# Attention and two feed-forward layers on one core: the 192-query softmax scaling moved from GpSimd to ScalarE and VectorE, its PSUM copies free to run on either, and every order computed anew

## The chip, the core and the metric

The kernel runs on one core of one Trainium2 chip. A core has a matrix engine (TensorE, PE in the profile), three elementwise engines (VectorE = DVE, ScalarE = ACT, GpSimd = POOL) and a queue, SyncE = SP, that starts DMA transfers. Each engine works through its own instructions strictly in order. The metric is the device time of one execution in microseconds (us); shorter is better.

## The reference

```python
def reference(q, k, v, moe_w_in, moe_w_out, moe2_w_in, moe2_w_out):   # q, k, v: (4, 8, 576, 64)
    scores = q @ k^T / sqrt(64), masked where query block i < key block j (blocks of 64)
    attn = softmax(scores) @ v
    x = attn, heads side by side            # (2304, 512)
    h = x @ w_in                            # 512 -> 2048
    x = (h * tanh(softplus(h))) @ w_out     # 2048 -> 512, "mish"
    h = max(x @ w2_in, 0)
    return (h * h) @ w2_out
```

All of it is float32, and the result is float32.

## The kernel before

**Tiling.** The 2304 tokens are cut into six chunks of 384. Chunks 0 and 1 are the first 192 queries of the four batches (two batches each); chunks 2 to 5 are the other 384 queries of one batch each. A chunk's attention has to be done before the chunk can go through layer one, and that before layer two. This makes 12 passes (a layer and a chunk each) in a fixed sequence. Within a pass the 2048 hidden columns are walked in 16 steps of 128: matrix products into `hp` (line 1063), the activation into `h` by ScalarE (line 1069, with 1088 in the first pass), the split of `h` into two float16 parts `g` (the high one by ScalarE, line 909, or GpSimd, line 910; the low one by VectorE, line 620), then products into four accumulators `acc` (line 1129). The products of the first pass read float32 directly (lines 1083 and 1098).

**Weights.** They arrive as 64-bit words, 1 MB a unit, 32 units (16 for each layer). A unit is decoded by one ScalarE instruction (line 934) and three of VectorE (937, 938, 940), and split into two float16 parts by ScalarE (948 and 909) and VectorE (620). In the first pass, layer one's decode, its split and the attention of chunk 1 run beside the matrix products.

**The 192-query attention** (`attention_lo`, 16 pairs of heads: eight in chunk 0, eight in chunk 1; in the texts a pair is called a head pair). For one of them: TensorE makes the scores (line 842); VectorE masks them and takes the row peaks (846 to 849); ScalarE takes three exponentials with their sums (852); VectorE adds a constant to the sums and takes the reciprocals (855, 857); three instructions of 192, 192 and 64 columns scale the exponentials by these (`scaled`, line 622; line 626 is its GpSimd form); TensorE turns the result round (865 to 868); ScalarE copies it out of PSUM (871); TensorE multiplies by v (880, 881); ScalarE copies that out of PSUM into `xs` (818 in `settle`).

**What sets the order.** While the program is built, a planner (`Sched`) is given every step with a duration in nanoseconds, places them one by one on the engines, and so fixes each engine's list. Some steps may go to one of several engines; the planner takes the one on which it reckons they end first (`choose`, table `ENG`). The instruction lists are then static. Its durations are the numbers in `c_act`, `c_dve`, `c_pool`; `L2_AT`, `S_AT`, `C0_AT`, `A_AT`, `ATT`, `LEAD`, `Sched.URGE`, `Sched.HYST` say from when and in what order of urgency things are wanted.

Of the kernel before, what the change touches and what calls it, by code (L numbers as in the profile page):

```python
# [26 lines left out]
ONE = None  # L27
# [17 lines left out]
LAG = 3  # L45
LOCK = False

# [9 lines left out]
def seg_len(tiles):  # L57
# [8 lines left out]
ENG = {"qkh": A + P, "v": V + P, "va": A, "rebias": A, "wh": A, "xh": A + P, "g1h": A + P, "g2h": A + P, "sq": A + P, "nsq": A,  # L66
       "pn": P, "ph": A, "pl": P + V}
EXTRA, EXTRAP = {"sv": 1, "st": 3}, {}
REBIAS = 2.0 ** -112
KBMAX = 207.4  # L70
DMAR = 290.0

# [4 lines left out]

L2_AT = [85000.0, 5000.0]
LEAD = [117000.0, 49680.0]
C0_AT, C1_AT, A_AT = 40000.0, 85000.0, [[0.0, 20000.0], [70000.0, 90000.0], [95000.0, 150000.0]]  # L80

# [29 lines left out]
class Sched:  # L111
# [15 lines left out]
    SHY = {}  # L127
    CONTEND = 0.5, 100.0, 0.3
    AHEAD = 1500.0
# [47 lines left out]
    def clock(self, t, start):  # L177

        left, now = t.dur, start
        while left > 0:  # L180
            k = int((now + self.PHASE) / self.TICK)
            rate = 1.0 if self.busy.get(k - 1, 0.0) >= self.DUTY * self.TICK else 2.0
            step = min(left * rate, (k + 1) * self.TICK - self.PHASE - now + 1e-3)
            self.busy[k] = self.busy.get(k, 0.0) + step / rate * t.rows
            left -= step / rate
            now += step
        t.dur = now - start
# [250 lines left out]
def c_f32(n):  # L438
    return 2 * max(107.0, 2.5 + n / 1.2)
# [7 lines left out]
def tile_attention_moe(ctx, tc, qk, qp, va, vd, w1, w2, out):  # L447
# [364 lines left out]
    def settle(src, av, n, xs, k, xo, sv):  # L812
# [4 lines left out]
        j = k if n > 192 else 2 * k + (xo > 0)  # L817
        sch.add("ACT", c_act(n, True, 0 if sv is ONE else 1), lambda: nc.scalar.activation(dst(), src(), AF.Copy, scale=scale()),
                r=r, w=[av, (xs, (k, xo))])
        if not whole:  # L820
# [3 lines left out]
    def attention_lo(b, h, x, xo, s_bank, av_bank):  # L824
# [45 lines left out]
        steps.append(sch.add("PE", 4 * 110.0, turn, r=[pf], w=[pp]))  # L870
        sch.add("ACT", c_act(448, True), lambda: nc.scalar.activation(pt.t, pp.t[:, 64:512], AF.Copy), w=[pp, pt])

        def second():
# [8 lines left out]

            step = sch.add("PE", 2 * c_f32(192) + c_f32(64) + 100, mm_av, r=[pt, vs], w=[av])
            step.rows = 0.8
# [38 lines left out]
    def decode(l, k, j):  # L923
# [9 lines left out]
        choose(ENG["rebias"], {  # L933
            "ACT": ("ACT", c_act(n), lambda: nc.scalar.activation(wf.t, high(), AF.Copy, scale=REBIAS), False),
            "POOL": ("POOL", c_pool(n, False), lambda: nc.gpsimd.tensor_scalar(wf.t, high(), REBIAS, 1.0, ALU.mult, ALU.mult), False),
# [500 lines left out]
```

## Time and profile before

| | |
|---|---|
| device time, median of 3 runs | 972.25 us (971.27 to 973.7) |
| the profiled execution: its device time | 972.16 us |
| its span, first to last instruction | 970.1 us |
| mean granted TensorE clock in it | 0.975 of full speed |
| busy: PE, DVE, ACT, POOL | 921.4, 598.0, 630.4, 131.6 us |

The span is 2.06 us shorter than the execution's own device time; that part lies around the instructions. A line "L626" is line 626 of the kernel. Busy time of PE is modelled from records of pipelined products, so a busy PE need not be a PE at full speed; the granted clock tells how fast it was allowed to run (1.00 is 2.4 GHz, 0.50 is 1.2 GHz).

### The profile page before, as it was taken

To read this page: it belongs to the slowest core of one execution; us is meant where nothing else is said; L and a number is where in the kernel's file an instruction comes from. 1 tells how busy PE (TensorE), PEld (TensorE's weight loads), DVE (VectorE), ACT (ScalarE), POOL (GpSimd) and SP (SyncE) were. 2 spreads that over 40 slices of the span, in tenths; PEclk is the share of its full clock that TensorE was granted. 3 is DMA by queue.
4 is the path that set the end of the run, shared out by engine and by line. 5 is a ranking of instruction groups with operands and counts; after the bars stand their busy time and mean duration, and the time that the engine had idled before them with its cause. 6 is when DMAs were issued, how large, how long until landed. Compare 5 with 4: busy or idle time off the path is not lost. (4 is left out here: it accounts for less than half of the span.)

```text
span 970.1 us, 15652 instructions
## 1 busy us (share of the span) xinstructions
PE 921.4 (95%) x5732; PEld 543.0 (56%) x5732; DVE 598.0 (62%) x1405; ACT 630.4 (65%) x1152; POOL 131.6 (14%) x192
## 2 busy tenths in 40 slices
PE   8688899899899999999999999999999999999997
PEld 7445465465455565555655655655556666666664
DVE  3767679999986757866685386677762341231211
ACT  5567898777776757798688677576784343353442
POOL 3212001123220111201221011011300100000000
PEclk9689989899999999999999999999999999999999
DMA  8467664685586655857444535676553221223222
GB/s 313 162 224 255 238 227 165 220 297 190 169 165 163 174 148 133 189 150 162 127 104 122 115 116 143 161 176 151 148 129 95 66 87 44 71 70 122 98 66 98
DMA packets 135725, 146.78 MB, mean 151 GB/s; under 512 B 105184, under 2 KB 110304, under 8 KB 131552
## 3 DMA queue, kind: packets, MB, share of 16 engines
q1 hardware_dynamic: 135648, 145.78, 52.1%
q8 instruction: 45, 0.74, 0.3%
q14 instruction: 32, 0.26, 0.1%
HBM read 106.43 MB, written 14.16 MB: 124 GB/s over the span
## 5 line engine op out<-in xcount | busy, mean ns | idle before, releaser
L1129 PE MATMUL acc<-g,ws 128*128 128x384 f16 x2112 | 431.6, 327 | 6.0 <-DVE g L620 3.9
L1129 PEld LDWEIGHTS <-ws 128*128 128x128 f16 x2112 | 204.6, 98 | 145.0 <-issue 9.1
L620 DVE SCALAR_TENSOR_TENSOR g<-h,cst,g 128x384 f16<-128x384 f32 x176 | 108.9, 621 | 208.1 <-ACT g L909 173.0
L1069 ACT ACTIVATE h<-hp,cst 128x384 f32<-128x384 f32 x176 | 101.1, 578 | 169.0 <-PE hp L1063 166.0
L1063 PE MATMUL hp<-x,first 128*128 128x384 f16 x960 | 201.2, 327 | 2.4 <-ACT h L1069 2.3
L1063 PE MATMUL hp<-x,late 128*128 128x384 f16 x864 | 180.8, 328 | 0.0
L1063 PEld LDWEIGHTS <-first 128*128 128x128 f16 x960 | 91.7, 98 | 66.4 <-issue 8.1
L1063 PEld LDWEIGHTS <-late 128*128 128x128 f16 x864 | 81.7, 98 | 58.1 <-issue 6.8
L910 POOL TENSOR_SCALAR g<-h,cst 128x384 f16<-128x384 f32 x77 | 60.7, 788 | 347.1 <-PE acc L1129 128.7
L726 ACT ACTIVATE pad<-pab,st,sq 128x320 f32<-128x320 f32 (+2 forms) x96 | 67.3, 703 | 30.0 <-DVE st L721 29.3
L620 DVE SCALAR_TENSOR_TENSOR pb<-pad,st,pb 128x384 f16<-128x384 f32 (+2 forms) x96 | 70.8, 749 | 17.8 <-ACT pb L744 16.4
L744 ACT ACTIVATE pb<-pad,st 128x384 f16<-128x384 f32 (+2 forms) x96 | 64.7, 713 | 15.4 <-ACT pad L726 4.9
L909 ACT ACTIVATE g<-h,cst 128x384 f16<-128x384 f32 x99 | 60.7, 613 | 19.5 <-PE acc L1129 17.7
L1083 PE MATMUL hp<-xs,first 128*128 128x384 f32 x128 | 56.1, 533 | 2.4 <-ACT h L1088 2.4
L1063 PE MATMUL hp<-x,ws 128*128 128x384 f16 x288 | 57.4, 326 | 0.0
L718 DVE TENSOR_REDUCE st<-pab 128x2 f32<-128x640 f32 (+2 forms) x48 | 49.9, 1040 | 3.9 <-PE pab L710 3.0
L1074 ACT ACTIVATE h<-h 128x384 f32<-128x384 f32 x86 | 44.0, 517 | 1.4
L1016 POOL TENSOR_SCALAR x<-xs,cst 128x384 f16<-128x384 f32 x30 | 23.3, 790 | 155.3 <-DVE cst L904 144.1
L626 POOL TENSOR_SCALAR pt<-pt,st 128x192 f32<-128x192 f32 (+1 forms) x48 | 26.6, 572 | 126.4 <-DVE st L857 72.0
L710 PE MATMUL pab<-q 64*128 64x320 f16 (+3 forms) x384 | 39.7, 308 | 2.2 <-DVE q L620 1.0
L1098 PE MATMUL acc<-h,late 128*128 128x384 f32 x96 | 39.3, 507 | 0.0
L1063 PEld LDWEIGHTS <-ws 128*128 128x128 f16 x288 | 27.0, 98 | 20.1 <-issue 2.9
(206 smaller groups left out, 1071.8 us busy)
## 6 DMA issues: line engine op xcount, KB each, us to landing
ws<-wspill SPq DMA_DIRECT2D x100, 512.0 KB, 3.7
raw<-in_w_dram SPq DMA_DIRECT2D x22, 1024.0 KB, 5.1
pad<-in_w_dram SPq DMA_DIRECT2D x10, 1024.0 KB, 4.9
wspill<-wn SPq DMA_DIRECT2D x18, 512.0 KB, 3.1
qk<-in_qp_dram SPq DMA_DIRECT2D x16, 480.0 KB, 4.1
vs<-in_va_dram SPq DMA_DIRECT2D x16, 320.0 KB, 4.2
out_dram<-ev SPq DMA_DIRECT2D x24, 192.0 KB, 2.0
vs<-in_qk_dram SPq DMA_DIRECT2D x10, 320.0 KB, 5.4
```

What stands on the lines that cost most here:

```text
L620: return sch.add("DVE", c_dve(n) + 62 * ap, lambda: nc.vector.scalar_tensor_tensor(dst(), a(), s() if ap else s, c(), op0, op1), r=r, w=w, ...
L710: nc.tensor.matmul(out=pp.t[:, hd, o:o + k1 - k0], lhsT=qh.t[rows, u, a:a + 128], rhs=qh.t[rows, w, nq + k0:nq + k1], start=p == 0, stop=p ...
L718: sch.add("DVE", c_dve(2 * (o1 - o0)), lambda: nc.vector.reduce_max(both(st, j, r0), pp.t[r0:, :, o0:o1], axis=AX.X), w=[(pp, 0), (st, j)])
L726: sch.add("ACT", c_act(o1 - o0, True, 3), lambda hd=hd: nc.scalar.activation(pf[hd].t[r0:, k0:k0 + o1 - o0], pp.t[r0:, hd, o0:o1], AF.Exp, ...
L744: sch.add("ACT", c_act(n, False, 1), lambda pb=pb, pv=pv, s=s: nc.scalar.activation(pb.t[:, 0:i + 1, 0, :], pv(), AF.Copy, scale=s()), r=[ ...
L909: "ACT": ("ACT", c_act(n, False, 1), lambda: nc.scalar.activation(dst(0), src(), AF.Copy, scale=s()), False),
L910: "POOL": ("POOL", c_pool(n, False), lambda: nc.gpsimd.tensor_scalar(dst(0), src(), s(), 1.0, ALU.mult, ALU.mult), False),
L1063: nc.tensor.matmul(out=hp.t[:, 0:n], lhsT=w.t[:, f % 2, a, 128 * k:128 * k + 128], rhs=x.t[:, c, k, 0:n], start=k == 0 and i == 0, stop=k ...
L1069: sch.add("ACT", c_act(n, True, 1), lambda: nc.scalar.activation(h.t[:, 0:n], hp.t[:, 0:n], (AF.Mish, AF.Relu)[l], scale=hs()), r=[(cst, ( ...
L1074: "ACT": ("ACT", c_act(n), lambda: nc.scalar.activation(hv(), hv(), AF.Square), False),
L1083: nc.tensor.matmul(out=hp.t[:, 0:n], lhsT=wf.t[:, 512 * (f % 2) + 128 * k:512 * (f % 2) + 128 * k + 128], rhs=xs.t[:, k, 0:n], start=k == ...
L1129: nc.tensor.matmul(out=acc.t[:, 0:n], lhsT=wo.t[:, f % 2, a, 128 * m:128 * m + 128], rhs=g.t[:, c, 0:n], start=f == 0 and i == 0, stop=f = ...
```

## The change

Three kinds of edit. First, `scaled` may no longer use GpSimd: table entry `pn` goes from GpSimd to ScalarE or VectorE. The two PSUM copies of the 192-query attention (`ptc`: the turned probabilities, 448 columns; `set`: the result, 192 columns) were ScalarE's alone and go through `copy`, which may choose VectorE. Second, numbers of the planner's model change: how VectorE and GpSimd hinder each other (`LOCK`, `CONTEND`), the DMA rate it reckons with, and a few durations. Third, the numbers that say when things are wanted were replaced, so that every engine's list is another.

```diff
-LOCK = False
+LOCK = True
...
-       "pn": P, "ph": A, "pl": P + V}
+       "pn": A + V, "set": A + V, "ptc": A + V, "ph": A, "pl": P + V}
...
-DMAR = 290.0
+DMAR = 360.0
...
-LEAD = [117000.0, 49680.0]
+LEAD = [111400.0, 111770.0]
...
-    CONTEND = 0.5, 100.0, 0.3
+    CONTEND = None
...
-        sch.add("ACT", c_act(n, True, 0 if sv is ONE else 1), lambda: nc.scalar.activation(dst(), src(), AF.Copy, scale=scale()),
-                r=r, w=[av, (xs, (k, xo))])
+        if sv is ONE:
+            copy(ENG["set"], n, dst, src, [], [av, (xs, (k, xo))], True)
+        else:
+            sch.add("ACT", c_act(n, True, 1), lambda: nc.scalar.activation(dst(), src(), AF.Copy, scale=scale()), r=r, w=[av, (xs, (k, xo))])
...
-        sch.add("ACT", c_act(448, True), lambda: nc.scalar.activation(pt.t, pp.t[:, 64:512], AF.Copy), w=[pp, pt])
+        copy(ENG["ptc"], 448, lambda: pt.t, lambda: pp.t[:, 64:512], [], [pp, pt], True)
...
-Sched.SHY={'DVE':1.5}
+Sched.SHY={}
...
-C0_AT = 27210.0
-A_AT = [[0.019, 18240.0], [55700.0, 114970.0]]
+C0_AT = 15160.0
+A_AT = [[0.013, 6840.0], [14100.0, 93900.0]]
...
-S_AT = [[38920.0, 4110.0], [19910.0, 4050.0]]
-Sched.URGE = 77120.0
+S_AT = [[39730.0, 3690.0], [23550.0, 3520.0]]
+Sched.URGE = 83480.0
```

Counted over the whole program, the 48 scaling instructions become 30 of VectorE (22 of 192 columns, 8 of 64) and 18 of ScalarE (10 and 8). Of the 16 copies of 448 columns VectorE gets 7, of the 16 of 192 columns 5. ScalarE's table loads go from 60 to 68. GpSimd's other work, all of which stands behind the scalings in its list, goes from 134 instructions to 115. No product of TensorE is added or taken away but two of the 13 that only fill its start.

The lists are another from the start, and three places matter. Lines after 820 stand two higher in the changed kernel. The first place is VectorE while the last head pairs of chunk 0 go through (`st` holds a head pair's sums and reciprocals, `pt` its probabilities, `first`, `late`, `raw` belong to weights that are decoded). Before:

```order
L940 SCALAR_TENSOR_TENSOR first_71<-raw0_67,first_71 128x1024
L847 TENSOR_REDUCE st_8_388<-spare_133 128x2
L848 TENSOR_REDUCE st_8_388<-spare_133 128x1
L849 TENSOR_SCALAR st_8_388<-st_8_388 128x3
L937 TENSOR_SCALAR late_70<-late_70 128x1024
L855 TENSOR_SCALAR st_7_368<-st_7_368 128x3
L938 SCALAR_TENSOR_TENSOR late_70<-raw1_68,late_70 128x1024
L857 RECIPROCAL st_7_368<-st_7_368 128x3
```

and in the changed kernel:

```order
L942 SCALAR_TENSOR_TENSOR first_71<-raw0_67,first_71 128x1024
L857 TENSOR_SCALAR st_6_305<-st_6_305 128x3
L598 COPY xs_0_260<-acc3_2_351 128x192
L859 RECIPROCAL st_6_305<-st_6_305 128x3
L939 TENSOR_SCALAR late_70<-late_70 128x1024
L627 TENSOR_SCALAR pt_128<-pt_128,st_6_305 128x192
L627 TENSOR_SCALAR pt_128<-pt_128,st_6_305 128x64
L857 TENSOR_SCALAR st_7_320<-st_7_320 128x3
L848 MEMSET spare_133 64x128
L859 RECIPROCAL st_7_320<-st_7_320 128x3
L940 SCALAR_TENSOR_TENSOR late_70<-raw1_68,late_70 128x1024
```

The scalings (L627) and copies (L598) now stand in VectorE's list between the weights' decode, and a wide decode row no longer stands between the sums and the reciprocal of the last head pair of chunk 0 (`st_7`).

The second place is TensorE at the start of the first pass (`spare` is a PSUM buffer of the attention, `xs_0` is chunk 0 as the first pass reads it). Before, up to the first product of the pass:

```order
L880 MATMUL spare_133<-pt_128,pb_127 64x192 x2
L881 MATMUL spare_133<-pt_128,pb_127 128x64
L842 MATMUL spare_133<-vs_129 128x192 x2
L842 MATMUL spare_133<-vs_129 128x64
L880 MATMUL spare_133<-pt_128,pb_127 64x192 x2
L881 MATMUL spare_133<-pt_128,pb_127 128x64
L1083 MATMUL hp0_131<-xs_0_281,first_71 128x384
```

and in the changed kernel:

```order
L867 MATMUL acc2_1_290<-ident_136,pt_128 128x128
L868 MATMUL acc2_1_290<-ident_136,pt_128 128x128
L869 MATMUL acc2_1_290<-ident_136,pt_128 128x2x64
L870 MATMUL acc2_1_290<-ident_136,pt_128 128x128
L882 MATMUL acc3_3_403<-pt_128,pb_127 64x192 x2
L883 MATMUL acc3_3_403<-pt_128,pb_127 128x64
L882 MATMUL spare_133<-pt_128,pb_127 64x192 x2
L883 MATMUL spare_133<-pt_128,pb_127 128x64
L1085 MATMUL hp0_131<-xs_0_260,first_71 128x384
```

Ten head pairs have their scores and nine are finished ahead of the first product of the pass before the change; with it nine have their scores and eight are finished. One pair of chunk 1 moves behind that product.

The third place is VectorE at the first `g` of the second pass (`wf`, `wn`, `late` are layer two's weights). Before:

```order
L955 TENSOR_SCALAR wst_895<-spare 128x2
L940 SCALAR_TENSOR_TENSOR wf<-raw_68,wf 128x1024
L956 TENSOR_SCALAR wst_895<-wst_895 128x2
L620 SCALAR_TENSOR_TENSOR g_1222<-h_1161,cst_1065,g_1222 128x384
L620 SCALAR_TENSOR_TENSOR late<-wf,us_1186,late 128x1024
L904 TENSOR_SCALAR us_1216<-wst_895 128x1
```

and in the changed kernel:

```order
L957 TENSOR_SCALAR wst_890<-spare 128x2
L942 SCALAR_TENSOR_TENSOR wf<-raw_68,wf 128x1024
L620 SCALAR_TENSOR_TENSOR g_1259<-h_1177,cst_1112,g_1259 128x384
L620 SCALAR_TENSOR_TENSOR g_1261<-h_1208,cst_1112,g_1261 128x384
L620 SCALAR_TENSOR_TENSOR g_1263<-h_1216,cst_1112,g_1263 128x384
L620 SCALAR_TENSOR_TENSOR wn_66<-wf,us_1164,wn_66 128x1024
```

Counted from the start of the list, 23 units of weights are decoded and 20 split ahead of this `g` before, 26 and 23 with the change; four reductions of 384 columns (L1108) and four others that stood ahead of it stand behind it.

## Rows read from the trace of the kernel before

**Rows 1.** Busy time of each engine in five stretches; columns as the first line says.

```profile
...
core 0: us, PE busy (x) PEld busy (x) DVE busy (x) ACT busy (x) POOL busy (x), PEclk, DMA share, GB/s
0.00:44.20 44.20, 31.79 (x164) 24.70 (x165) 22.28 (x70) 24.64 (x79) 13.33 (x37) 0.81 0.71 251
44.20:174.80 130.60, 116.57 (x412) 67.82 (x412) 100.47 (x208) 102.65 (x168) 17.02 (x23) 0.92 0.61 217
174.80:280.20 105.40, 96.72 (x592) 54.76 (x592) 101.29 (x215) 79.46 (x128) 26.59 (x26) 0.95 0.68 217
280.20:403.60 123.40, 117.92 (x850) 67.62 (x847) 88.52 (x219) 82.90 (x174) 19.42 (x26) 1.00 0.64 158
403.60:970.00 566.40, 558.42 (x3726) 328.08 (x3720) 285.40 (x696) 340.73 (x606) 55.29 (x80) 1.00 0.44 115
```

**Rows 2.** Timeline of PE: start us, us, what, and idle time before it with its releaser.

```profile
...
27.71 0.43 PE L881 MATMUL acc<-pt,pb 128*128 128x64 f32 x2
34.14 0.47 PE L865 MATMUL acc<-ident,pt 128*128 128x128 f32 x1 [5.99 <-POOL pt L626]
...
44.23 1.59 PE L1083 MATMUL hp<-xs,first 128*128 128x384 f32 x2
```

**Rows 3.** Timeline of VectorE ahead of that stall.

```profile
...
31.18 0.16 DVE L855 TENSOR_SCALAR st<-st 128x3 f32<-128x3 f32 x1
31.30 1.23 DVE L938 SCALAR_TENSOR_TENSOR late<-raw,late 128x1024 uint32<-128x1024 uint32 x1
32.44 0.17 DVE L857 RECIPROCAL st<-st 128x3 f32<-128x3 f32 x1
```

**Rows 4.** Timeline of GpSimd, its first six scalings and a later six.

```profile
...
11.08 2.35 POOL L626 TENSOR_SCALAR pt<-pt,st 128x192 f32<-128x192 f32 x6 [9.47 <-DVE st L848]
...
32.80 4.47 POOL L626 TENSOR_SCALAR pt<-pt,st 128x192 f32<-128x192 f32 x6 [7.03 <-DVE st L855]
```

**Rows 5.** Busy time in windows of 10 us.

```profile
...
20.00:30.00 10.00, 7.90 (x56) 5.33 (x54) 5.64 (x15) 6.92 (x21) 1.43 (x5) 0.98 0.35 132
30.00:40.00 10.00, 4.26 (x15) 2.31 (x15) 7.47 (x15) 5.75 (x15) 4.47 (x6) 0.53 0.70 243
40.00:50.00 10.00, 9.06 (x26) 5.80 (x27) 5.74 (x12) 5.27 (x11) 0.00 (x0) 0.62 0.58 208
50.00:60.00 10.00, 6.39 (x17) 3.42 (x16) 7.56 (x11) 6.23 (x10) 3.84 (x3) 0.72 0.73 256
```

**Rows 6.** Groups of VectorE by form: busy us, mean ns of one, idle before.

```profile
...
L938 DVE SCALAR_TENSOR_TENSOR wf<-raw,wf 128x1024 uint32<-128x1024 uint32 x11 | 14.0, 1268 | 0.0
L940 DVE SCALAR_TENSOR_TENSOR wf<-raw,wf 128x1024 uint32<-128x1024 uint32 x11 | 13.6, 1235 | 0.0
L620 DVE SCALAR_TENSOR_TENSOR wn<-wf,us,wn 128x1024 f16<-128x1024 f32 x10 | 13.1, 1310 | 0.0
...
L937 DVE TENSOR_SCALAR first<-first 128x1024 uint32<-128x1024 uint32 x8 | 5.7, 717 | 2.1 <-ACT first L934 2.1
...
L847 DVE TENSOR_REDUCE st<-spare 128x2 f32<-128x384 f32 x9 | 4.9, 542 | 0.1
...
L1108 DVE TENSOR_REDUCE xm<-xs 128x1 bf16<-128x384 f32 x4 | 2.2, 546 | 0.0
...
L848 DVE TENSOR_REDUCE st<-spare 128x1 f32<-128x64 f32 x9 | 1.9, 212 | 0.3 <-PE spare L881 0.3
```

**Rows 7.** Groups of GpSimd by form.

```profile
...
L626 POOL TENSOR_SCALAR pt<-pt,st 128x192 f32<-128x192 f32 x32 | 18.1, 579 | 126.4 <-DVE st L857 72.0 <-ACT h L1088 20.3 <-DVE wst L956 12.0
```

**Rows 8.** Waits of VectorE in the first pass: us in total, times, longest us.

```profile
...
DVE spare L846 <- PE spare L881: 12.9, 6, 4.7
```

**Rows 9.** Waits of PE in the first pass, same columns.

```profile
...
PE spare L867 <- POOL pt L626: 1.7, 2, 1.3
```

**Rows 10.** Groups of ScalarE by form.

```profile
...
L726 ACT ACT_TABLE_LOAD x22 | 28.2, 1283 | 6.1 <-DVE cst L899 3.5 <-DVE st L721 2.3
...
L818 ACT ACTIVATE xs<-spare 128x192 f32<-128x192 f32 x12 | 3.9, 329 | 12.0 <-PE spare L949 4.7 <-DVE st L847 3.0 <-DVE spare L846 1.9
```

More of the change, by code (lines that the diff above doesn't have):

```diff
@@ L181, in clock @@
             k = int((now + self.PHASE) / self.TICK)
-            rate = 1.0 if self.busy.get(k - 1, 0.0) >= self.DUTY * self.TICK else 2.0
+            rate = 1.0 if k > 2 and self.busy.get(k - 1, 0.0) >= self.DUTY * self.TICK else 2.0
             step = min(left * rate, (k + 1) * self.TICK - self.PHASE - now + 1e-3)
@@ L881, in mm_av @@
                 nc.tensor.matmul(out=av.t[:, 128:192], lhsT=vs.t[:, 128:256], rhs=pt.t[:, 0:64], start=False, stop=True)
-            step = sch.add("PE", 2 * c_f32(192) + c_f32(64) + 100, mm_av, r=[pt, vs], w=[av])
+            step = sch.add("PE", c_f32(192) + c_f32(64) + 200, mm_av, r=[pt, vs], w=[av])
             step.rows = 0.8
@@ L933, in decode @@
         choose(ENG["rebias"], {
-            "ACT": ("ACT", c_act(n), lambda: nc.scalar.activation(wf.t, high(), AF.Copy, scale=REBIAS), False),
+            "ACT": ("ACT", c_act(n) + 90.0, lambda: nc.scalar.activation(wf.t, high(), AF.Copy, scale=REBIAS), False),
             "POOL": ("POOL", c_pool(n, False), lambda: nc.gpsimd.tensor_scalar(wf.t, high(), REBIAS, 1.0, ALU.mult, ALU.mult), False),
@@ L947, in split @@
         sq, us, sc = (R[x].new() for x in ("wsq", "us", "sc"))
-        sch.add("ACT", c_act(n) + 190.0, lambda: nc.scalar.activation(sq.t, wf.t, AF.Square, scale=2.0 ** -13, accum_out=us.t[:, 1:2]), r=[wf], w=[sq, (us, 1)])
+        sch.add("ACT", c_act(n) + 93.0, lambda: nc.scalar.activation(sq.t, wf.t, AF.Square, scale=2.0 ** -13, accum_out=us.t[:, 1:2]), r=[wf], w=[sq, (us, 1)])
         step = sch.add("PE", 110.0, lambda: nc.tensor.matmul(out=sc.t[:, 0:1], lhsT=onesq, rhs=us.t[:, 1:2].bitcast(BF16)[:, 1:2], start=True, stop=True),
@@ L1352 @@
 ATT = [[2, 2, 0, 0.0, 1.2], [3, 2, 1, 1.1, 2.6], [4, 5, 7, 0.5, 2.2], [5, 5, 8, 2.0, 3.6]]
-L2_AT = [89170.0, 2960.0]
+L2_AT = [92220.0, 2850.0]
 W_AT = [[[4300.0, 4600.0], [47800.0, 6800.0]]]
-C0_AT = 27210.0
-A_AT = [[0.019, 18240.0], [55700.0, 114970.0]]
-ATT = [[2, 2, 0, 0.0, 1.309], [3, 2, 1, 0.832, 1.394], [4, 5, 7, 0.015, 2.865], [5, 5, 8, 0.0, 4.407]]
+C0_AT = 15160.0
+A_AT = [[0.013, 6840.0], [14100.0, 93900.0]]
+ATT = [[2, 2, 0, 0.021, 1.144], [3, 2, 1, 0.943, 1.494], [4, 5, 7, 0.0, 4.142], [5, 5, 8, 0.027, 4.334]]
 Sched.SLACK = 0.445
-Sched.HYST = 21950.0
+Sched.HYST = 25790.0
 def setup():
```

## The prediction

> **What bounds the kernel now.** I read the stretches first [rows 1]. They are cut at the first product of the first pass (44.2 us), the first activation of the second pass (174.8), a step in the middle of the third pass (280.2) and the start of the fifth (403.6). In the last stretch TensorE is busy 558.4 of 566.4 us at a granted clock of 1.00: there it alone sets the time, and the change adds no product to it. From 280.2 to 403.6 it is busy 117.9 of 123.4, also at 1.00. So the end of the kernel stands at a nearly fixed distance behind 280.2, and what can be won or lost lies ahead. In the third stretch VectorE is busy 101.3 of 105.4 us, 96%, and TensorE 96.7: VectorE is the limit. In the second nobody is full: VectorE 100.5 and ScalarE 102.7 of 130.6 us, TensorE 116.6 by its records, at 0.92. The first 44.2 us are the emptiest: VectorE 22.3, ScalarE 24.6.
>
> Then I read the timeline where the head is emptiest. TensorE ends a product at 28.14 (27.71 and 0.43) and starts the next at 34.14, after 5.99 us of waiting for a scaling on GpSimd [rows 2]. The reader is to see who was late there: not GpSimd alone. VectorE adds the constant to the sums at 31.18, decodes weights for 1.23 us, and only then takes the reciprocal, at 32.44 [rows 3]; GpSimd starts at 32.80. But then six scalings take it 4.47 us, where its first six took 2.35 [rows 4]. The hole has a second price: the granted clock reads 0.98 in the 10 us before it, then 0.53, 0.62 and 0.72 [rows 5], near the lower of the two levels, 1.2 and 2.4 GHz.
>
> **The change part by part.** The sum is made for one point, the one at 280.2 us, where VectorE is the limit: its time is VectorE's work up to there plus VectorE's idle time up to there. Before, work is 22.28 + 100.47 + 101.29 = 224.0 us, so idle time is 56.2: 21.9 in the head, 30.1 in the first pass, 4.1 in the third stretch [rows 1].
>
> *Work added to VectorE.* 30 scalings and 12 copies. A scaling of the very kind (one tensor, one scalar per row, buffer to buffer) stands in the trace with 1024 columns at 0.717 us [rows 6] and with 3 columns at 0.16 [rows 3]; on the line between them 192 columns are 0.26 and 64 are 0.19, so 22 x 0.26 + 8 x 0.19 = 7.2 us. Bounds: 30 x 0.16 = 4.8, and 30 x 0.579, what GpSimd took on the wide ones [rows 7], = 17.4. I take the line, since the engine and kind of operation are the same. For a read of PSUM, 64 columns are 0.212 and 384 are 0.542 [rows 6], so 192 are 0.34, 448 are 0.61, and the copies 5 x 0.34 + 7 x 0.61 = 6.0 us (2.5 if each went at the 64-column row; 7.3 if each at 0.61). The rows overlap: the one that starts at 31.30 and lasts 1.23 ends 0.09 after the next has started [rows 3]; 42 instructions take 42 x 0.09 = 3.8 off. Net 13.2 - 3.8 = 9.4 us.
>
> *Work that is only moved.* Three units of weights (decode 0.717 + 1.268 + 1.235, split 1.310, together 4.5 us each [rows 6]) go from behind the second pass's first g to ahead of it, and eight reductions (four of them 0.546 each) the other way. Both are over by 280.2 in either list. The units' loads and spills, 1.5 MB each, join a stretch whose DMA share is 0.61 [rows 1], so 4.5 MB more over some 130 us, 35 GB/s on 217, has room. By 280.2 the new list also has five more instructions of the next attention done (384 to 640 columns; by the line of the PSUM reads about 3.5 us) and TensorE has 15 more products behind it. The last stretch has 558.42 us for 3726 products [rows 1], 0.15 each, so these are a credit of 2.2 us.
>
> *Idle time taken away.* In the head a scaling now follows its reciprocal on the same engine, or goes to ScalarE: the way through GpSimd is gone, and with it 4.47 us for two head pairs. The last pair of chunk 0 no longer has a decode row between sums and reciprocal. And one head pair less stands ahead of the first pass. VectorE has the copies and scalings to fill its gaps with. I take half of the head's 21.9 us: 11; bounds 6 and 22. In the first pass 12.9 of VectorE's 30.1 idle us are six waits for TensorE to make room for the next scores [rows 8], and TensorE in turn waits for GpSimd's scalings (1.7 us at one line, the longest of several [rows 9]). With the hole gone and the clock up these shrink, and VectorE has more in its list. Bounds: 30, as now, and 10 (the third stretch's 4% of some 130 us is 5; the ends of the pass add to it). The middle is near 21, and I take that. The third stretch keeps 4.
>
> *Waits added.* A scaling on VectorE waits for ScalarE's exponentials through its reciprocal, and behind it stand decode rows, for which the weights' split and the float32 products of the first pass wait. On ScalarE 18 scalings come (0.329 us for a 192-column copy of PSUM [rows 10], so about 6) and 12 copies go (about as much by the same row and the wider ones). Its 8 more table loads, 8 x 1.283 = 10.3 us [rows 10], lie mostly behind 280.2, where it is idle 40.5 of 123.4 and 225.7 of 566.4 us [rows 1]; that idle time hides them. If it did not, they would cost up to 10.3; I charge 1.5. The two filling products that go stand ahead of everything; I cost them at nothing, and at 0.15 us a product they could not be worth more than 0.3.
>
> *Sum.* 224.0 + 9.4 + 3.5 + (11 + 21 + 4) = 272.9 against 280.2 is -7.3; credit -2.2; table loads +1.5: -8.0. The span of 970.1 becomes 962.1, and with the 2.06 around it the execution is **964.2 us**. The profiled execution's 972.16 is the median of the runs (972.25) within 0.1.
>
> *A rule of the skill beside it.* The two groups of six scalings, 2.35 and 4.47 us, differ by what VectorE did meanwhile: in the second it decodes [rows 3, 4]. The Trainium skill (SBUF — State Buffer, section "Who interferes with whom") says that VectorE, in its two-port modes or with two operands from SBUF, and GpSimd exclude each other for a whole instruction. By that rule the trace agrees on GpSimd's side, VectorE would get time back as well (the rival "More" below), and a scaling on VectorE would block GpSimd where that has work at the time; in the new list all its other work stands later.
>
> **The rivals.**
>
> *Slower: VectorE's list becomes the bound of the first pass.* VectorE takes 9.4 us more in order, each scaling stands ahead of decode rows, and a late exponential then holds up decode, split and the products that wait for them. For it: VectorE and ScalarE are both near 78% there already, and list order has cost them the rest. Against: 30.1 us of slack. Each idle us of the first pass is one us of time: 21 gives 964.2, 29 gives 972, and from 32 on it is slower by over 0.3%. With 36, 979 us.
>
> *No change: the way through GpSimd was not the cause.* The hole of 6 us was opened by VectorE's late sums and reciprocal; GpSimd came 0.36 us after it [rows 3]. If the head keeps some 18 of its 21.9 idle us, because the new list also has decode rows between, the time is 964 + 7 = 971.
>
> *More: the head and first pass both close up.* If idle time falls to 8 and 12 us, it is 3 + 9 = 12 us less, 952. For it speaks the lost clock: three windows at 0.53, 0.62 and 0.72 hold 19.7 us of busy TensorE [rows 5], about 7 us of which (4.26 x 0.47 + 9.06 x 0.38 + 6.39 x 0.28) a full clock would have spared. VectorE rows that no longer share their time with GpSimd's would do it too: if VectorE lost as much as GpSimd did, 48 x (0.579 - 2.35/6) = 9 us, 955.
>
> **Chances.** The forecast (958 to 969) 0.48, more 0.16, no change 0.19, slower 0.17. 0.3%, 2.9 us, is about what a measurement of this kernel can tell from no change. Faster by over that: 0.64; within: 0.19; slower: 0.17. The likeliest is 964; the range reaches from 954 to 977.
>
> **What would show it.** Right: no wait of TensorE over 3 us between 20 and 40 us; the first product of the first pass near 36 instead of 44.23 us; a granted clock over 0.8 from 30 to 60; VectorE busy over 80% from there to the second pass, and over 95% up to the point that was at 280.2; a DVE scaling of 192 columns near 0.26 us. Wrong: VectorE idle over 30 us between the first product of the first pass and the second pass, waiting for ScalarE's exponentials or TensorE's scores; a scaling near 0.5 us; or TensorE waits behind 403.6 that were not there, by ScalarE's table loads.

## The result, and the profile after

The changed kernel takes 956.28 us (median of 4 runs, 954.85 to 959.01) against 972.63 for the kernel before on the same chip: a ratio of 0.9836, 95% interval 0.9807 to 0.9865. It is faster by 16 us. The prediction said 964.2, with a range of 954 to 977. The profiled execution took 954.89 us, its span is 953.1 and its mean granted clock 0.991.

The five stretches, cut at the same steps as in [rows 1], as the windows view has them for the changed kernel:

```profile
...
core 0: us, PE busy (x) PEld busy (x) DVE busy (x) ACT busy (x) POOL busy (x), PEclk, DMA share, GB/s
0.00:29.53 29.53, 23.04 (x146) 18.05 (x146) 20.34 (x78) 20.29 (x73) 1.06 (x10) 1.00 0.95 349
29.53:158.20 128.67, 111.62 (x425) 66.82 (x425) 116.29 (x247) 118.86 (x196) 2.11 (x2) 0.95 0.71 257
158.20:262.50 104.30, 99.44 (x627) 56.59 (x627) 95.49 (x229) 78.54 (x135) 18.49 (x20) 0.98 0.63 189
262.50:384.50 122.00, 117.07 (x845) 68.28 (x841) 86.06 (x215) 84.89 (x173) 15.11 (x19) 1.00 0.65 161
384.50:953.10 568.60, 555.25 (x3698) 326.32 (x3696) 277.87 (x681) 347.83 (x612) 49.90 (x74) 1.00 0.42 113
```

The step that stood at 280.2 us is now at 262.5. From there to the end it is 690.6 us, before 970.1 - 280.2 = 689.9. So all of the gain lies ahead of that point (the step is the same activation of the third pass in every kernel). VectorE's work up to it is 20.34 + 116.29 + 95.49 = 232.1 us, before 224.0. Its idle time, span less busy in each of the three stretches, is 9.2 + 12.4 + 8.8 = 30.4, before 21.9 + 30.1 + 4.1 = 56.2.

The timeline of TensorE where [rows 2] showed the hole of 6 us. The longest wait between 20 and 40 us is 0.79; the first product of the first pass starts at 29.53 instead of 44.23:

```profile
...
22.37 0.55 PE L882 MATMUL acc<-pt,pb 128*64 128x192 f32 x4 [0.79 <-DVE pt L598]
...
29.53 0.86 PE L1085 MATMUL hp<-xs,first 128*128 128x384 f32 x2
```

The windows of 10 us that answer to [rows 5]. The clock is 1.00 in all of them, and VectorE is busy 8.86 us at 20 to 30, where it was 5.64. The last but one number is the DMA engines' share:

```profile
...
20.00:30.00 10.00, 7.81 (x52) 5.12 (x51) 8.86 (x26) 8.82 (x30) 0.00 (x0) 1.00 1.04 397
30.00:40.00 10.00, 9.23 (x39) 5.53 (x38) 8.47 (x18) 8.31 (x15) 0.00 (x0) 1.00 0.78 297
40.00:50.00 10.00, 9.49 (x31) 5.49 (x30) 7.79 (x16) 9.42 (x16) 0.00 (x0) 1.00 0.93 326
50.00:60.00 10.00, 10.00 (x43) 6.27 (x42) 9.25 (x16) 9.44 (x16) 0.00 (x0) 1.00 0.86 326
```

The new rows among the groups of VectorE (busy us, mean ns of one), with a decode row for comparison with [rows 6]:

```profile
...
L942 DVE SCALAR_TENSOR_TENSOR wf<-raw,wf 128x1024 uint32<-128x1024 uint32 x11 | 13.7, 1248 | 0.0
...
L627 DVE TENSOR_SCALAR pt<-pt,st 128x192 f32<-128x192 f32 x22 | 6.3, 314 | 0.1
...
L598 DVE COPY pt<-spare 128x448 f32<-128x448 f32 x5 | 3.1, 623 | 0.8 <-PE spare L951 0.8
...
L627 DVE TENSOR_SCALAR pt<-pt,st 128x64 f32<-128x64 f32 x8 | 2.0, 256 | 0.0
...
L598 DVE COPY xs<-spare 128x192 f32<-128x192 f32 x4 | 1.4, 355 | 1.1 <-PE spare L883 0.8 <-PE spare L951 0.3
```

The scalings that went to ScalarE take 461 and 342 ns there.

VectorE's largest wait in the first pass (us, times, longest), which answers to [rows 8]: 5.7 us where there were 12.9.

```profile
...
DVE spare L848 <- PE spare L883: 5.7, 6, 3.2
```

### The profile page after: what moved, and what is told of

It reads as the page before. It is cut to its first block, busy times and chain, and to the rows that moved or that the text cites. A ratio compares the mean times of both kernels' runs of the same rounds, so it can differ in the third digit from the quotient of the medians.

```text
span 953.1 us, 15648 instructions
## 1 busy us (share of the span) xinstructions
PE 906.4 (95%) x5730; PEld 536.1 (56%) x5730; DVE 596.1 (63%) x1447; ACT 650.4 (68%) x1185; POOL 86.7 (9%) x125
## 5 line engine op out<-in xcount | busy, mean ns | idle before, releaser
L1065 PE MATMUL hp<-x,first 128*128 128x384 f16 x960 | 196.8, 326 | 0.6 <-DVE cst L1033 0.3
L912 POOL TENSOR_SCALAR g<-h,cst 128x384 f16<-128x384 f32 x70 | 49.6, 710 | 360.7 <-PE acc L1131 147.8
L911 ACT ACTIVATE g<-h,cst 128x384 f16<-128x384 f32 x106 | 65.0, 615 | 12.7 <-PE acc L1131 11.7
L1085 PE MATMUL hp<-xs,first 128*128 128x384 f32 x128 | 52.8, 504 | 0.0
L1076 ACT ACTIVATE h<-h 128x384 f32<-128x384 f32 x91 | 47.1, 517 | 1.3
L1018 POOL TENSOR_SCALAR x<-xs,cst 128x384 f16<-128x384 f32 x24 | 20.6, 872 | 249.7 <-DVE cst L1054 154.1
L726 ACT ACT_TABLE_LOAD x25 | 32.1, 1283 | 15.7 <-DVE st L721 10.8
```

Of the source, the lines that this page charges most:

```text
L726: sch.add("ACT", c_act(o1 - o0, True, 3), lambda hd=hd: nc.scalar.activation(pf[hd].t[r0:, k0:k0 + o1 - o0], pp.t[r0:, hd, o0:o1], AF.Exp, ...
L911: "ACT": ("ACT", c_act(n, False, 1), lambda: nc.scalar.activation(dst(0), src(), AF.Copy, scale=s()), False),
L1065: nc.tensor.matmul(out=hp.t[:, 0:n], lhsT=w.t[:, f % 2, a, 128 * k:128 * k + 128], rhs=x.t[:, c, k, 0:n], start=k == 0 and i == 0, stop=k ...
L1076: "ACT": ("ACT", c_act(n), lambda: nc.scalar.activation(hv(), hv(), AF.Square), False),
L1085: nc.tensor.matmul(out=hp.t[:, 0:n], lhsT=wf.t[:, 512 * (f % 2) + 128 * k:512 * (f % 2) + 128 * k + 128], rhs=xs.t[:, k, 0:n], start=k == ...
```

## The experiments

Twelve kernels, each timed against the kernel before on its own chip, where that took 971.92 us (e1 to e4), 971.38 (e5 to e8) and 972.97 (e9 to e12). The changed kernel was timed only beside the 972.63 above, so a comparison with it goes across chips. "First product" is the start of the first product of the first pass; the last column is the place of the step that stood at 280.2. These two are from the profiled execution, which need not be the median one.

| kernel | median us | ratio to before, 95% interval | first product | step |
|---|---|---|---|---|
| before | 972.63 | | 44.2 | 280.2 |
| after | 956.28 | 0.9836 (0.9807 to 0.9865) | 29.5 | 262.5 |
| e1: lists of before, scalings on VectorE | 964.08 | 0.9938 (0.9917 to 0.9959) | 43.9 | 271.3 |
| e2: lists of after, scalings on GpSimd | 976.6 | 1.0052 (1.0028 to 1.0076) | 33.7 | 281.9 |
| e3: after, GpSimd busy beside it | 962.14 | 0.9924 (0.9898 to 0.995) | 33.4 | 270.1 |
| e4: before, 60 filling products | 969.62 | 0.9977 (0.9959 to 0.9995) | 42.5 | 279.0 |
| e5: after, copies on ScalarE | 962.81 | 0.9914 (0.9886 to 0.9943) | 33.0 | 266.7 |
| e6: after, the wanted-when numbers of before | 971.42 | 0.9994 (0.9977 to 1.0011) | 31.2 | 276.5 |
| e7: before, the new choice of engines alone | 978.36 | 1.0061 (1.0041 to 1.0081) | 31.8 | 268.6 |
| e8: before, 105 filling products | 972.33 | 0.9999 (0.9983 to 1.0015) | 43.4 | 279.9 |
| e9: before, decode rows behind the chain | 974.95 | 1.0017 (1.0 to 1.0034) | 46.0 | 282.4 |
| e10: e1 and e9 together | 967.11 | 0.9952 (0.993 to 0.9974) | 46.9 | 274.5 |
| e11: before, 185 filling products | 971.9 | 0.9992 (0.9978 to 1.0007) | 43.8 | 280.4 |
| e12: after, the same shift at its second hole | 963.6 | 0.99 (0.987 to 0.9929) | 32.0 | 271.5 |

**e1 and e2: the engine and the lists apart.** Each instruction keeps its place; only the engine that scales is another, in e1 in the lists of before:

```diff
-        choose(ENG["pn"], {
+        t = choose(ENG["pn"], {
...
+        swap.append((t, lambda: nc.vector.tensor_scalar(v(), v(), s(), None, ALU.mult)))
...
     seq = sch.run(order)
+    for t, fn in swap:
+        t.fn = fn
```

e2 does the same with GpSimd's form (`nc.gpsimd.tensor_scalar`) in the lists of after. Expected of e1:

> The lists of before, but the 48 scalings are VectorE's, each at the place in the order at which GpSimd's stood. Theory A (the way through GpSimd is what cost): the 6 us hole of TensorE at 28 us shrinks to 4 or less, the clock falls less, 962 to 968 us. Theory B (the new lists are what gained, the engine is secondary): within 3 us of before, 970 to 975, because VectorE's list still has the decode rows in front; or slower, since VectorE has 8 us more to do in lists that were not planned for it.

Of e2:

> The lists of after, but all 48 scalings are GpSimd's, each at the place in the order at which VectorE's or ScalarE's stood. Theory A: most of the gain is lost, 966 to 973 us, with TensorE waiting for scalings of 0.4 to 0.75 us. Theory B: 955 to 960 us, because the lists keep the decode rows out of the way.

Measured: the engine alone gives 8 us in the old lists (e1). The new lists with the scalings on GpSimd cost 5 (e2; its 12 copies are still VectorE's, so this is not the lists quite alone, and e1 has all 48 scalings on VectorE, where the changed kernel has 18 on ScalarE). Together they give 16: with the new lists the engine is worth 20. TensorE's timeline of e1 shows that the hole stays as long as it was although GpSimd has no scaling left:

```profile
...
34.29 0.44 PE L868 MATMUL acc<-ident,pt 128*128 128x128 f32 x1 [5.89 <-DVE pt L628]
```

VectorE's timeline of e1 shows what took GpSimd's place. The reciprocal is taken at 32.56, as before (32.44), but then a decode row stands in the list, and the scalings start at 33.83, where GpSimd had started at 32.80 [rows 4]:

```profile
...
32.70 1.22 DVE L943 SCALAR_TENSOR_TENSOR late<-raw,late 128x1024 uint32<-128x1024 uint32 x1
33.83 0.70 DVE L628 TENSOR_SCALAR pt<-pt,st 128x192 f32<-128x192 f32 x3
```

The first pass of e1 in the windows view:

```profile
...
43.90:167.60 123.70, 113.78 (x412) 67.07 (x412) 104.28 (x229) 102.84 (x169) 2.60 (x2) 0.93 0.64 230
```

Of the 8.9 us by which e1 is ahead at the step, 6.9 come from the first pass, 123.7 us against 130.6 [rows 1], 1.7 from the third stretch and 0.3 from the head. In e2 the first product comes at 33.7, and from 20 us to there TensorE's longest wait is 1.19 us: in the new lists the hole is closed even with GpSimd. But the first pass takes 144.6:

```profile
...
33.70:178.30 144.60, 120.04 (x424) 69.71 (x425) 114.60 (x230) 117.03 (x190) 23.77 (x26) 0.90 0.63 222
```

and TensorE's waits in it name GpSimd's scalings, 11.5 us in these three lines alone:

```profile
...
PE spare L871 <- POOL pt L628: 4.9, 6, 1.1
PE spare L872 <- POOL pt L628: 4.6, 4, 2.0
...
PE spare L870 <- POOL pt L628: 2.0, 3, 1.1
```

VectorE's idle time in the four kernels, us, worked out as above from windows cut at the same steps:

| | head | first pass | third stretch | its work |
|---|---|---|---|---|
| before | 21.9 | 30.1 | 4.1 | 224.0 |
| e1 | 17.2 | 19.4 | 2.7 | 231.9 |
| e2 | 15.7 | 30.0 | 8.4 | 227.8 |
| after | 9.2 | 12.4 | 8.8 | 232.1 |

The engine takes 10.7 us of VectorE's idle time out of the first pass in the old lists and 17.6 in the new ones, for 7.9 and 4.3 us more work up to the step. The first pass itself gets shorter by 6.9 (130.6 to 123.7) and 15.9 us (144.6 to 128.7).

**e3: what GpSimd's work does to VectorE.** After, with a scaling on GpSimd of a buffer that nobody reads, beside each of the 48:

```diff
+        beside[t] = lambda: nc.gpsimd.tensor_scalar(idle[:, 0:n], idle[:, 0:n], s(), 1.0, ALU.mult, ALU.mult)
...
             t.fn()
+            if t in beside:
+                beside[t]()
```

> After, and beside each scaling GpSimd scales a buffer of its own of the same size that nobody reads (48 rows more for GpSimd, no wait for them). If GpSimd's rows take time from VectorE's: VectorE's decode and scaling rows in the first 160 us get longer, 4 to 9 us in all, and the time rises to 959 to 965. If they do not: 955 to 958, and the decode rows keep their 1.22 us.

Measured: 962.14, some 6 us over after, with no wait that names those rows. The groups of VectorE in e3:

```profile
...
L947 DVE SCALAR_TENSOR_TENSOR first<-raw,first 128x1024 uint32<-128x1024 uint32 x5 | 6.1, 1225 | 0.0
...
L627 DVE TENSOR_SCALAR pt<-pt,st 128x192 f32<-128x192 f32 x22 | 7.3, 359 | 0.1
...
L627 DVE TENSOR_SCALAR pt<-pt,st 128x64 f32<-128x64 f32 x8 | 2.6, 327 | 0.0
```

The decode rows with two inputs keep their duration: 1225 ns in this group, 1217 in the same group of after. Not each of them has a GpSimd row beside it, so I also counted row by row in the trace of e3: the 10 that overlap one of GpSimd's scalings take 1.232 us in the mean, the other 34 take 1.227. GpSimd pays: its scalings of 192 columns take 1.28 us beside a row of VectorE with two inputs of 1024 columns (9 of them), 0.52 otherwise (23). VectorE's scalings grow from 314 to 359 and from 256 to 327 ns, 22 x 0.045 + 8 x 0.071 = 1.6 us. VectorE's work up to the step is 235.1, 3.0 more, its idle time 35.0, 4.6 more. Of that 2.7 are in the head, where the clock fell:

```profile
...
20.00:30.00 10.00, 8.23 (x38) 5.79 (x35) 7.85 (x23) 6.95 (x26) 5.84 (x9) 0.62 1.01 378
30.00:40.00 10.00, 10.00 (x32) 5.43 (x31) 6.73 (x16) 8.04 (x16) 2.71 (x5) 0.69 0.54 182
```

1.6 us of longer scalings are shown. Why the head lost 3.9 us is not: it lost its clock there, and which small delay came first I did not separate. The head of one and the same program moves too: in e12, which is after up to some 100 us, the first product came 2.5 us later than in after.

**e4, e8, e11: the clock behind the hole.** Before, with filling products in front of the turn that TensorE waits for: 60 and 105, then 185 to cover the hole. e8 and e11 write a free bank; in e4 the bank was one that TensorE first had to wait for, 3.8 us.

```diff
+            if t is turns[7]:
+                for _ in range(185):
+                    nc.tensor.matmul(out=hps[1][:, 0:64], lhsT=ones, rhs=ones[:, 0:64], start=True, stop=True)
             t.fn()
```

> Before, with 60 small products that nobody reads put into TensorE's list in front of the turn of the eighth head pair, where it sat idle for 6 us. If the clock that fell there is a large part of the price: granted clock near 1.00 from 30 to 60 us, 3 to 7 us faster than before, 966 to 970. If waits alone set the head: within 2 us of before.

> Before, with 105 small products that nobody reads in front of the turn of the eighth head pair, now into a PSUM bank that is free there, so that they do not wait for anybody (the 60 of the earlier run waited 3.8 us first). If the clock is a large part of the price of the hole: granted clock over 0.9 from 30 to 60 us, the hole as long as before, 965 to 969 us. If the clock costs little there, since the other engines are waited for anyway: 969 to 972.

> Before, with 185 filling products into a free bank in TensorE's hole of 6 us (105 of them had lasted 3.23 us); no list is changed otherwise. If the hole's second price, the clock that falls behind it, is what costs the time: clock over 0.85 from 30 to 50 and 965 to 968. If the clock falls because of the thin work that follows, or costs little: 0.6 to 0.7 there as before and 970 to 973.

Measured: e4 2 us faster, with its clock at 0.67 to 0.68 from 30 to 60, so these 2 us are not the clock's; e8 and e11 no change. In e8 the 105 left 2.92 us of the hole and the clock at 0.62 to 0.70. In e11 the hole is filled, and these are its windows, to be held against [rows 5]:

```profile
...
20.00:30.00 10.00, 9.75 (x141) 7.60 (x138) 5.71 (x16) 7.34 (x22) 1.50 (x5) 1.00 0.36 126
30.00:40.00 10.00, 7.02 (x120) 4.95 (x116) 7.73 (x15) 5.79 (x16) 4.46 (x6) 0.81 0.72 243
40.00:50.00 10.00, 9.52 (x28) 6.13 (x29) 6.13 (x11) 5.58 (x14) 0.00 (x0) 0.68 0.61 218
50.00:60.00 10.00, 6.52 (x16) 3.71 (x15) 6.74 (x11) 5.45 (x8) 3.85 (x3) 0.66 0.65 244
```

The clock is 0.81 instead of 0.53 at 30 to 40, about as before in the 20 us behind, and the first product comes at 43.8 instead of 44.2. So the hole's second price, "about 7 us", was not there to be had by closing the hole: most of it was reckoned for 40 to 60 us, and there the clock stays low with the hole filled. What a full clock from 40 to 60 would give is not shown, since no fill brought it about.

**e9, e10: taking the decode out of the chain.** In before (e9) and in e1 (e10), the wide rows of VectorE and ScalarE between the scores and the turn of that head pair go behind the turn, with what depends on them:

```diff
+    for p in (7,):
+        first, last = turns[p]
+        i, j = seq.index(first), seq.index(last)
+        late, now = [], []
+        for t in seq[i:j + 1]:
+            own = first.idx <= t.idx <= last.idx
+            wide = t.eng in ("DVE", "ACT") and t.dur > 600.0
+            behind = any(d in late for d in t.deps | t.after)
+            (late if not own and (wide or behind) else now).append(t)
+        seq[i:j + 1] = now + late
```

> The lists of before, the scalings on GpSimd as before; only the wide rows (decode, over 0.6 us) that VectorE and ScalarE have between the scores and the turn of the eighth head pair, the one for which TensorE waits 6 us, are put behind that turn, with what depends on them. Theory, the list made the hole: some 4 to 5 us of decode rows lie in that pair's chain, so the hole of 6.0 us falls under 2, the first product of the first pass comes near 40 (43 to 44 before), the granted clock is over 0.8 from 30 to 50, and the time is 965 to 969 against 972. Rival, the way through GpSimd made it: the hole keeps over 4 us and the time 971 to 973.

> The same shift of the decode rows, with the scalings of before's lists emitted on VectorE, which by itself gave 964.1. If closing the hole and taking the scalings off GpSimd are two separate gains: 958 to 961. If they are one and the same, or what the hole gives is lost again in the first pass as with the new lists and GpSimd: 963 to 966.

Measured: e9 is not faster, and neither theory held (974.95; e10, at 967.11, lies 1 us outside both of its ranges). The wait for the scalings falls from 5.99 to 2.16 us, but TensorE then waits 7.36 for a product that the weights' split needs:

```profile
...
29.89 0.47 PE L867 MATMUL acc<-ident,pt 128*128 128x128 f32 x1 [2.16 <-POOL pt L626]
...
38.63 0.16 PE L952 MATMUL spare<-us,onesq 128*128 128x1 bf16 x1 [7.36 <-ACT wsq L951]
38.66 0.45 PE L867 MATMUL spare<-ident,pt 128*128 128x128 f32 x1
...
45.97 0.95 PE L1086 MATMUL hp<-xs,first 128*128 128x384 f32 x1
```

ScalarE's timeline in e9 shows why: the decode now starts at 29.77, and the squares for the split wait 4.46 us for the decoded unit.

```profile
...
29.77 1.17 ACT L937 ACTIVATE first<-raw 128x1024 f32<-128x1024 f32 x1
...
37.43 1.06 ACT L951 ACTIVATE wsq<-late 128x1024 bf16<-128x1024 f32 x1 [4.46 <-DVE late L943]
```

The chain of the head pair and the decode of the first units were both late, and putting either first only changes which one TensorE waits for. e10 says the same with the other engine: its first pass takes 170.8 - 46.9 = 123.9 us, as in e1, and its head is 3 us longer. What the engine gives in the first pass doesn't depend on the head.

What the new lists do there instead can be read in two places. The first is TensorE's own list. In e9 the turn of the eighth head pair, the last of chunk 0, comes at 29.89, and the first product of the pass still only at 45.97: the split's first product (L952) and the whole ninth head pair stand between them. In the changed kernel both stand behind the first product of the pass, which starts at 29.53:

```profile
...
30.69 0.16 PE L951 MATMUL spare<-us,onesq 128*128 128x1 bf16 x1 [0.29 <-ACT pt L854]
...
35.94 0.30 PE L867 MATMUL spare<-ident,pt 128*128 128x128 f32 x1 [0.47 <-DVE pt L627]
```

The ninth head pair's turn is hardly earlier than before, 35.94 against 36.77. All seven kernels with new lists (after, e2, e3, e5, e6, e7, e12) have the first product ahead of both, at 29.5 to 33.7; all seven with the lists of before have it behind both, at 42.5 to 46.9. So a good part of the 14.7 us by which the first product is earlier is work that moved behind it.

The second place is the decode, which starts earlier. Before, ScalarE's first decode row:

```profile
...
24.34 1.17 ACT L934 ACTIVATE first<-raw 128x1024 f32<-128x1024 f32 x1
```

and in the changed kernel:

```profile
...
15.52 1.12 ACT L936 ACTIVATE first<-raw 128x1024 f32<-128x1024 f32 x1 [1.08 <-DMA raw<-in_w_dram]
```

The windows of 4 us tell from where. Before, the DMA engines stood nearly still at 24 to 28 us (share 0.03), VectorE had 0.72 us of work in the 4 us ahead of that, and its decode came later, in the hole:

```profile
...
20.00:24.00 4.00, 3.75 (x29) 2.24 (x28) 0.72 (x3) 2.70 (x11) 0.30 (x2) 0.96 0.82 313
24.00:28.00 4.00, 4.00 (x29) 3.08 (x28) 2.97 (x7) 2.61 (x6) 1.12 (x3) 1.00 0.03 14
```

In the changed kernel the loads fill that time, and both engines decode in it:

```profile
...
20.00:24.00 4.00, 2.79 (x21) 2.07 (x20) 4.00 (x13) 4.00 (x17) 0.00 (x0) 1.00 1.08 394
24.00:28.00 4.00, 3.31 (x23) 1.92 (x21) 3.74 (x11) 3.28 (x12) 0.00 (x0) 1.00 1.01 396
```

But the earlier decode is not what the closed hole needs. In e7 (below) the decode starts almost as late as before and the DMA share is 0.32 from 20 to 30, and still TensorE's longest wait between 20 us and its first product, at 31.8, is 1.75:

```profile
...
23.27 1.15 ACT L936 ACTIVATE first<-raw 128x1024 f32<-128x1024 f32 x1
```

e7's clock then falls to 0.54 from 30 to 40, where after keeps 1.00. Whether the earlier decode is what keeps it up no run tries alone.

**e5: the copies.** After's lists, with the 12 copies on ScalarE again:

```diff
-        return choose(engs, {
+        t = choose(engs, {
...
+        copies.append((t, lambda: nc.scalar.activation(dst(), src(), AF.Copy)))
...
+    for t, fn in copies:
+        t.fn = fn
```

> The lists of after, but the 12 copies out of PSUM that VectorE had (7 of 448, 5 of 192 columns) are ScalarE's, each at its place in the order. If the copies carry part of the gain: ScalarE, about 92% busy in the first pass, gets some 5.5 us more, and the time is 958 to 963. If only the scalings matter: 955 to 958.

Measured: 962.81, and its interval lies above that of after. In the profile 3.5 us are lost in the head and 1.5 in the first pass, and 0.8 are won back in the third stretch. But of the 3.5 some 2.4 came with a load: TensorE waits 2.47 us for queries and keys at 17.6 us, in after 1.25; its clock then reads 0.51 at 18 to 20 us, in after 1.00, and the products of these queries and keys end at 20.8 instead of 18.4. e12 shows the same delay at the same place with the program of after. So the copies on VectorE are worth 2 (4.2 at the step less 2.4) to 6.5 us (by the medians, across chips).

**e6 and e7: the engines with the old numbers.** e6 is after with the numbers of before that say when things are wanted (`C0_AT`, `A_AT`, `S_AT`, `LEAD` and the others of the diff); e7 is before with the new table entries and the two copies as `copy`. In both the planner makes new lists.

> The changed kernel with its engines and its planner's durations, but the numbers that say when things are wanted are those of before, so the planner makes other lists. If the engines carry the gain (they gave 8 us in the lists of before): 955 to 965. If the new numbers do: 965 to 972.

> Before with the new engine choices alone (scalings on ScalarE or VectorE, copies on either): the planner's durations and its numbers are those of before, the lists are planned for the choice. If it suffices that the planner knows of the choice: clearly under the 964 of the unplanned exchange, 955 to 961, with the first product of the first pass before 36 us. If the durations and numbers are needed: 961 to 968.

Measured: neither is faster than before; e6 falls in the range for the new numbers, e7 outside both of its ranges. The head is short in both (31.2 and 31.8), and e7 shows that the new engines alone let the planner close it. Each loses later: e6 between the thirteenth activation of the first pass and the first of the second (123.4 to 172.1 us, where after takes from 129.2 to 158.2), with TensorE waiting 4.0 us for one step of ScalarE's (`nsq`) and 3.4 for the squares of the weights' split; e7 is 16 us ahead of before at 387.4 us, and then takes 105.4 us for what after does in 79.1; TensorE's longest waits there, 4.2 and 3.8 us, stand at products of a later attention (`pab`). One of e7's four executions took 2401 us; its ratio is that of the other three, with a median of 977.86.

**e12: the second hole of the changed kernel.** TensorE has one more thin stretch, 100 to 118 us, where the chain of the fourteenth head pair runs between decode and split rows. The edit is that of e9 with pair 13.

> The kernel after the change, with the same kind of shift at its largest remaining hole, 104 to 117 us: the wide rows in the chain of the fourteenth head pair go behind its turn. If these rows hold up the chain and TensorE is what the pass waits for: waits of TensorE there fall from some 8 to 4 us, clock over 0.8 instead of 0.50 at 110 to 118, and 951 to 954. If VectorE and ScalarE, which are nearly full there, are what the pass waits for: 955 to 959, with the work only put off.

Measured: 963.6, slower than after and outside both ranges. The windows of after:

```profile
...
100.00:110.00 10.00, 3.99 (x24) 2.63 (x23) 8.40 (x22) 9.89 (x22) 0.00 (x0) 0.83 0.38 152
110.00:120.00 10.00, 7.01 (x22) 4.81 (x22) 6.65 (x31) 8.31 (x14) 0.00 (x0) 0.50 0.44 157
120.00:130.00 10.00, 10.00 (x40) 6.02 (x39) 9.64 (x16) 9.96 (x17) 0.00 (x0) 0.98 0.43 159
```

and of e12:

```profile
...
100.00:110.00 10.00, 8.34 (x36) 5.00 (x35) 5.52 (x27) 8.01 (x17) 0.00 (x0) 1.00 0.60 220
110.00:120.00 10.00, 1.70 (x8) 1.15 (x8) 7.76 (x19) 7.69 (x17) 0.00 (x0) 0.64 0.13 52
120.00:130.00 10.00, 6.16 (x19) 4.20 (x20) 6.56 (x25) 8.38 (x13) 0.00 (x0) 0.51 0.43 157
```

The hole is later and wider: TensorE is busy 16.2 us of 30 instead of 21.0, though e12 comes to these windows some 4 us late (its ninth activation stands at 89.8, after's at 85.5). The work that was put off came back as a wait for ScalarE (3.7 us for a scaling, 5.1 for squares). From the ninth activation of the first pass to the thirteenth e12 takes 49.2 us, after 43.7. So no version that I ran beats the changed kernel.

## Why the prediction was right, and where it was not

**The number.** The way it moved was right, its size was half: 8.0 us were forecast, 16.4 measured. 956.3 lies in the stated range of 954 to 977 but below the forecast's own band of 958 to 969, in the part of the rival "more", which had a chance of 0.16.

**What bounds the kernel: right.** The distance from the step to the end is 690.6 us against 689.9, in the experiments 688.2 to 692.5 except where the late attention lost time (e7, 708.4). The credit of 2.2 us for work already done and the charge of 1.5 for table loads, -0.7 together, came out as +0.7. The last stretch is 568.6 us with 3698 products, before 566.4 with 3726 [rows 1]: the credit is there (28 x 0.15 = 4.2 us), and is more than used up by small waits of TensorE, the largest of them for ScalarE's exponentials, whose line loads a table 25 times instead of 22 [rows 10]. The waits' view of after there, in us, times and longest:

```profile
...
PE pab L710 <- ACT pad L726: 2.3, 3, 1.1
```

The prediction had named such waits as a sign against it; they are here, and small. Whether the loads cause them I did not try.

**The terms of the sum.** Predicted 272.9 for the step, measured 262.5. Of the 10.4 us, 8.6 are one term, mis-sized: VectorE's idle time in the first pass, taken as 21 between bounds of 10 and 30, is 12.4. I took the middle of the bounds; the waits for room for the next scores fell from 12.9 to 5.7 [rows 8], and most of the others with them. The head's idle time was taken as 11 and is 9.2. The third stretch's was taken as unchanged at 4 and is 8.8, the one term that came out worse; e2 has 8.4 there, so it belongs to the new lists. TensorE is now the fuller one there (99.44 of 104.30, VectorE 95.49), so "VectorE is the limit" no longer holds in that stretch. The work was taken as 12.9 more and is 8.1 more; that these two misses of 4.8 cancel is luck. In its parts the scalings were a little longer than the line gave, 314 and 256 ns against 260 and 190, and the copies as estimated, 623 and 355 against 610 and 340. The overlap was too small: in e1, the groups

```profile
...
L628 DVE TENSOR_SCALAR pt<-pt,st 128x192 f32<-128x192 f32 x32 | 9.0, 309 | 0.3
...
L628 DVE TENSOR_SCALAR pt<-pt,st 128x64 f32<-128x64 f32 x16 | 3.9, 244 | 0.0
```

sum to 32 x 0.309 + 16 x 0.244 = 13.8 us, and VectorE's busy time grew by 7.9. That is 0.12 of overlap for each instruction (shorter decode rows are in it too), where I had 0.09.

**The hole: wrong in its cause.** The step "the way through GpSimd is gone, and with it 4.47 us" failed. The rows themselves allow less: GpSimd starts at 32.80 and the hole ends at 34.14 [rows 2, 4], so only 1.3 of the 4.47 us lie in the hole; the 4.3 us ahead of the reciprocal at 32.44 are VectorE's and ScalarE's. e1 takes GpSimd out and the hole is 5.89 us, since a decode row now stands ahead of the scalings; e9 takes the decode out of the chain, and the next wait is 7.36; e2 puts GpSimd back into the new lists, and the longest wait is 1.19. The rival "the way through GpSimd was not the cause" had the better reading of the hole, but not its time: the new lists close the head. Two things in them are seen, the first product ahead of the ninth head pair and of the weights' split, and in after the earlier decode (15.52 against 24.34). The prediction named the ninth pair in one short sentence and passed over the split and the decode; how much each is worth stays open, but e7 closes the hole without the earlier decode. So the head's term, 11 against 9.2, came out near for another reason than the one given. The price of the lost clock was laid to the hole, and filling the hole did not win it back (e11).

**Where GpSimd did cost time: the first pass.** The prediction had it in one clause, by a wait of 1.7 us [rows 9], and it is the larger part of what the engine gives: 10.7 us of VectorE's idle time in the old lists (e1), 17.6 in the new (e2 against after). The waits that name GpSimd in before are small (1.7 us, and two lines of 1.4). I read it so that each of them delayed the turn, with it the room for the next scores, and so VectorE: VectorE's waits for that room fall from 12.9 us to 10.0 in e1, and from 11.9 in e2 to 5.7 in after. The rest of the idle time is spread over smaller waits, and no run follows it one by one.

**The rivals.** "Slower": by the second pass e2 has lost the head's gain (178.3 us there, before 174.8), as that rival feared for after, but through GpSimd's scalings and not through VectorE's list. "More", with 952, had idle times of 8 and 12 for the head and first pass. They came out at 9.2 and 12.4, so in its terms it is nearer than the forecast. From 952 to the profiled 954.9 it is 1.6 us of these two and 1.4 behind the step; one of its reasons, the lost clock, was not won back by filling the hole (e11). The part of it that is the rule of the Trainium skill (SBUF — State Buffer, section "Who interferes with whom") did not carry on VectorE's side: by e3, VectorE's rows with two inputs lose nothing to GpSimd's scalings (1.232 us beside them, 1.227 otherwise), so there were no 9 us to get back. On GpSimd's side e3 agrees with it (1.28 us against 0.52).

**What the views were to show.** Right: no wait over 3 us between 20 and 40; the clock over 0.8 from 30 to 60; VectorE over 80% in the first pass (116.29 of 128.67, 90%). Off: the small waits in the last stretch; the first product at 29.5, not 36; the scaling at 0.314 us, not 0.26; and VectorE over 95% up to the point, which is 92% (95.49 of 104.30).

**Still open.** How the 8 us between e1 and after share out among TensorE's new order in the head, the earlier decode, the copies and the other lists, since e2 and e6 show that the parts don't add.

## What to carry to other kernels

A wait that names an engine need not be that engine's price: before crediting the hole to it, see how much of its work lies inside the hole, put the operation on another engine in the same lists, and look at what stands ahead of it there. When two chains are late at once (here a softmax and a decode), putting one ahead of the other can only move the wait (5.99 us became 2.16 and 7.36); look also at what else stands in the waiting engine's list ahead of the product you want early. And a new choice of engine and a new order can be worth less one by one (8, -5) than together (16).

## What the runs showed of the hardware

- VectorE beside GpSimd: decode rows with two inputs of 1024 columns did not grow when GpSimd scaled at the same time (e3: 1.227 us without, 1.232 with), while GpSimd's scalings of 192 columns beside them went from 0.52 to 1.28 us. VectorE's own scalings by a scalar per row did, from 314 to 359 and from 256 to 327 ns. In e2 GpSimd's own scalings took 757 ns for 192 columns, in before 579 [rows 7].
- The same lists, other landings: e12's program is that of after up to some 100 us, and still its first product of the first pass came at 32.0 instead of 29.5. TensorE waited 2.43 us for queries and keys at 17.3 us, in after 1.25, and its clock then read 0.50 at 18 to 20 us, in after 1.00, so that their products took 3.55 us instead of 1.93. With the DMA share at 1.0 from 10 to 30 us the head is sensitive to when a load lands, as it was not before (one wait of 1.2 us for a load).
- Filling products of 64 columns held the granted clock while they lasted: from 27.5 to 33.1 us in e11, with 1.00 in the windows of 2 us from 28 to 34, where before had 0.64 at 30 to 32 and 0.50 at 32 to 34. From 38 to 44 it read 0.50 in both.
